# One 2 MB weight load requested as 32 partitions and 96 partitions

## The chip, the cores and the metric

The kernel runs on one core of a Trainium2 chip. The time is device microseconds of one execution, the median of several runs. The span in a profile is about 2 us shorter (77.6 us in a run of 79.66). In the profile's lines, PE is the matrix engine's matmuls and PEld its weight loads, DVE, ACT and POOL are the vector, scalar and general engines, and SP issues most requests. A request is one DMA instruction. A bulk request gives 16 completion increments in these traces, read here as one from each DMA engine whose share has landed.

## The reference, cut to what matters

```python
xn = layernorm(x)                                   # one token, D = 512
q  = xn @ wq                                        # wq: 512 x 4096, 4 MB
# 32 query heads, 8 key/value heads, the last W = 4096 positions of a cache of 65536
o  = softmax(q k^T / sqrt(128)) v
out = x + o @ wo + xn + sigmoid(xn . w_r) * ((silu(xn @ w_gate) * (xn @ w_up)) @ w_down)
```

One token meets 30.7 MB of weights and cache rows. Each is read once, so there is little arithmetic per byte.

## The kernel before

`wq` lies as [128 partitions, 4 rows, 4096]. Its first half is 16 KB per partition. The request for it, and the one for `x`, are moved by hand to the start of the program, ahead of the barrier that all engines pass ("the head barrier"). They reach SP and ACT as their first instructions.

```python
    KH = KT // 2                                              # 2
    wq_v = A_wq.rearrange("(p kt) n -> p kt n", kt=KT)
    ...
            for i in [i for i, o in enumerate(blk.instructions) if o.name in ahead][::-1]:
                ins = blk.instructions.pop(i)
                at = next(k for k, o in enumerate(head) if o.engine == ins.engine and isinstance(o, mybir.InstDrain))
                head.insert(at, ins)
    ...
    t_wq = [early(nc.sync, "wq0", wq_sb[:, 0:KH, :], wq_v[:, 0:KH, :])]       # ahead of the barrier
    t_x = early(nc.scalar, "x", xrow[:], A_x.rearrange("a b d -> (a b) d"))
    ...
    t_wq.append(dma(sy, "wq1", wq_sb[:, KH:, :], wq_v[:, KH:, :]))            # behind it
    t_k = sum([pair("k", k_sb, A_k_cache, a, b) for a, b in steps([0, 1, 2, 4, 6, 8])], [])
    ...
    for kh in range(2):
        PE.need(t_wq[kh], t_ps0)                              # the projection waits for its half of wq
    ...
    # then v, w_gate, w_up, wo, w_down, all from SP, long ahead of their use
```

## Time and profile before

| | |
|---|---|
| time, median of 3 | 79.57 us (79.53 to 79.73) |
| span in the profile | 77.6 us |
| moved from HBM | 30.67 MB, 395 GB/s over the span |
| first packet of wq | 1.04 us |
| last completion increment of w_down | 75.61 us |

The first thing to look at is the page's row of GB/s in 40 slices of 1.94 us, here of the kernel before:

```profile
GB/s 136 405 406 422 414 422 427 422 469 414 439 456 439 405 422 414 439 439 431 405 410 422 481 414 422 413 449 399 451 406 451 413 422 414 481 361 413 355 29 1
```

The row is flat from its second entry to the last three. This kernel ends when its bytes have passed: 30.67 MB at some 425 GB/s are 72 of its 77.6 us. For the experiments below, the same in three stretches of the kernel before (length, busy time and number of instructions of PE, PEld, DVE, ACT and POOL, PE's granted clock, DMA share, GB/s):

```profile
2.00:7.00 5.00, 0.26 (x4) 0.21 (x4) 2.76 (x6) 2.72 (x5) 2.89 (x5) 1.00 0.99 420
7.00:11.00 4.00, 2.80 (x20) 1.01 (x20) 2.81 (x14) 0.20 (x1) 0.00 (x0) 1.00 0.99 426
11.00:16.00 5.00, 3.56 (x26) 1.07 (x24) 0.60 (x5) 1.17 (x2) 0.00 (x0) 1.00 0.99 418
```

The first stretch is wq's first half, the second its second half, the third the first cache rows. All three move 418 to 426 GB/s with the DMA share at 0.99.

### The profile page before, as it was taken

To read this page: it belongs to the slowest core of one execution; us is meant where nothing else is said; L and a number is where in the kernel's file an instruction comes from. 1 tells how busy PE (TensorE), PEld (TensorE's weight loads), DVE (VectorE), ACT (ScalarE), POOL (GpSimd) and SP (SyncE) were. 2 spreads that over 40 slices of the span, in tenths; PEclk is the share of its full clock that TensorE was granted. 3 is DMA by queue.
4 is the path that set the end of the run, shared out by engine and by line. 5 is a ranking of instruction groups with operands and counts; after the bars stand their busy time and mean duration, and the time that the engine had idled before them with its cause. 6 is when DMAs were issued, how large, how long until landed. Compare 5 with 4: busy or idle time off the path is not lost.

```text
span 77.6 us, 1640 instructions
## 1 busy us (share of the span) xinstructions
PE 58.4 (75%) x642; PEld 30.6 (39%) x642; DVE 44.2 (57%) x96; ACT 30.4 (39%) x41; POOL 10.0 (13%) x22
## 2 busy tenths in 40 slices
PE   0010797759997997997996796677887889898891
PEld 0010401346785575765864234222222344243240
DVE  2763910177656956868883652989879545600302
ACT  2760101404397698599568016143333322000001
POOL 3950000001020210201205900000000000000000
PEclk9999999999999999999999999999999999999999
DMA  6999999999999999999999999999999999989900
GB/s 136 405 406 422 414 422 427 422 469 414 439 456 439 405 422 414 439 439 431 405 410 422 481 414 422 413 449 399 451 406 451 413 422 414 481 361 413 355 29 1
DMA packets 2745, 30.72 MB, mean 396 GB/s; under 512 B 307, under 2 KB 438, under 8 KB 822
## 3 DMA queue, kind: packets, MB, share of 16 engines
q1 hardware_dynamic: 2738, 30.67, 94.0%
q8 instruction: 2, 0.03, 0.2%
q14 instruction: 1, 0.01, 0.0%
q10 hardware_dynamic: 4, 0.00, 0.0%
HBM read 30.67 MB, written 0.00 MB: 395 GB/s over the span
## 4 chain that ended last, share of the span: by engine, by line
DMA 64%; PE 20%; ACT 6%; DVE 4%; issue 2%; SPq 1%
DMA k_sb<-in_B_w_down_dram 50%; DMA wq_sb<-in_A_wq_dram 14%; PE ps L367 10%; ACT kT L342 6%; PE ps L541 3%; PE ps L376 3%; PE ps L295 2%; DVE kin L334 2%; PE ps L307 1%; SPq L199 1%; DVE kT L339 1%; DVE qpad L312 1%; DVE kT L568 1%; SPq L84 0%; SPq L101 0%
## 5 line engine op out<-in xcount | busy, mean ns | idle before, releaser
L342 ACT COPY kT<-ps 128x1024 bf16<-128x1024 bf16 x19 | 18.6, 1016 | 9.5 <-PE ps L367 9.4
L367 PE MATMUL ps<-perm_bf,kin 128*128 128x128 bf16 x256 | 18.7, 231 | 1.5 <-DVE kin L334 1.0
L367 PEld LDWEIGHTS ps<-perm_bf,kin 128*128 128x128 bf16 x256 | 15.8, 104 | 5.9 <-issue 4.7
L334 DVE COPY kin<-k_sb 128x2048 bf16<-128x2048 bf16 x16 | 10.9, 687 | 2.6 <-PE ps L367 2.6
L339 DVE COPY kT<-ps 128x1024 bf16<-128x1024 bf16 x13 | 9.0, 692 | 4.4 <-PE ps L367 3.8
L462 ACT CAST pvS<-ps 128x512 bf16<-128x512 f32 x8 | 4.7, 586 | 10.0 <-PE ps L468 10.0
L376 PE MATMUL ps<-kT,qAB 128*32 128x512 bf16 x68 | 7.1, 407 | 1.9 <-ACT kT L342 1.9
L191 PE MATMUL ps<-zmov,zst 128*128 128x512 bf16 x32 | 7.9, 381 | 0.0
L327 POOL COPY qAB<-qpad 128x64 bf16<-128x64 bf16 x8 | 3.6, 445 | 32.6 <-PE ps L376 32.6
L442 DVE COPY vin<-v_sb 128x2048 bf16<-128x2048 bf16 x8 | 5.5, 685 | 1.1 <-PE ps L477 0.9
L448 DVE COPY vin<-v_sb 128x2048 bf16<-128x2048 bf16 x8 | 5.5, 683 | 0.0
L477 PE MATMUL ps<-vin,pTcur 128*32 128x512 bf16 x32 | 3.2, 386 | 2.6 <-ACT pvS L462 2.2
L569 ACT CAST kT<-ps 1x256 bf16<-1x256 f32 x1 | 0.4, 362 | 11.4 <-PE ps L541 11.4
L489 PE MATMUL ps<-zmov,zst 128*128 128x512 bf16 x16 | 4.7, 376 | 0.0
L295 PE MATMUL ps<-wq_sb,xnT 128*1 128x512 bf16 x32 | 3.8, 620 | 0.6 <-DMA wq_sb<-in_A_wq_dram 0.6
L191 PEld LDWEIGHTS ps<-zmov,zst 128*128 128x128 bf16 x32 | 2.7, 97 | 3.7 <-issue 1.3
L251 PE MATMUL ps<-ident_bf,xn_row 1*128 1x1 bf16 x4 | 0.3, 166 | 5.2 <-DVE xn_row L246 5.2
L312 DVE COPY qpad<-ps 128x16 bf16<-128x16 bf16 x4 | 0.5, 170 | 5.4 <-PE ps L307 5.4
L555 DVE TENSOR_TENSOR kT<-ps,kT 128x512 f32<-128x512 f32 x1 | 0.7, 692 | 5.0 <-PE ps L536 5.0
L376 PEld LDWEIGHTS ps<-kT,qAB 128*32 128x32 bf16 x68 | 1.9, 93 | 4.1 <-issue 1.8
L477 PEld LDWEIGHTS ps<-vin,pTcur 128*32 128x32 bf16 x32 | 1.1, 93 | 6.0 <-DVE vin L442 5.5
L483 PE MATMUL ps<-vin,pTcur 128*32 128x512 bf16 x32 | 3.2, 387 | 0.3 <-DVE vin L448 0.2
(96 smaller groups left out, 54.7 us busy)
## 6 DMA issues: line engine op xcount, KB each, us to landing
v_sb<-in_A_v_cache_dram SPq DMA_DIRECT2D x4, 2048.0 KB, 38.2
k_sb<-in_A_k_cache_dram SPq DMA_DIRECT2D x3, 2048.0 KB, 23.3
wq_sb<-in_A_wq_dram SPq DMA_DIRECT2D x2, 2048.0 KB, 9.1
k_sb<-in_A_wo_dram SPq DMA_DIRECT2D x2, 2048.0 KB, 34.7
k_sb<-in_A_k_cache_dram SPq DMA_DIRECT2D x2, 1024.0 KB, 13.9
wq_sb<-in_B_w_gate_dram SPq DMA_DIRECT2D x1, 1792.0 KB, 43.0
wq_sb<-in_B_w_up_dram SPq DMA_DIRECT2D x1, 1792.0 KB, 46.9
k_sb<-in_B_w_down_dram SPq DMA_DIRECT2D x1, 896.0 KB, 38.7
```

Source lines behind the costliest of these rows:

```text
L191: te.matmul(ps[:, 7, :], lhsT=zst[:], rhs=zmov[:], start=True, stop=True)
L295: ins = te.matmul(ps[32 * c:32 * c + 1, hf, :], lhsT=xnT[:, kt:kt + 1], rhs=wq_sb[:, kt, (4 * hf + c) * 512:(4 * hf + c + 1) * 512], start ...
L334: ve.tensor_copy(out=kin[:, 2 * h:2 * h + 2, :], in_=k_sb[:, g, 2 * h:2 * h + 2, :]).then_inc(s_c[h], 1)
L339: ve.tensor_copy(out=kT[:, b, :], in_=tp[:, b, :]).then_inc(s_ev[b], 1)
L342: ac.copy(out=kT[:, b, :], in_=tp[:, b, :]).then_inc(s_ev[b], 1)
L367: ins = te.transpose(tp[:, b, k * P:(k + 1) * P], kin[:, b, k * P:(k + 1) * P], perm_bf[:])
L376: ins = te.matmul(sc[32 * cq:32 * cq + 32, e, :], lhsT=qAB[:, e, :], rhs=kT[:, b, :].rearrange("d (k h q) -> d h k q", h=2, q=PH)[:, e], s ...
L442: ve.tensor_copy(out=vin[:, 0].rearrange("p (q k) d -> p q (k d)", q=4), in_=v_in[:, :, 0:4 * DH]).then_inc(s_va, 1)
L448: ve.tensor_copy(out=vin[:, 1].rearrange("p (q k) d -> p q (k d)", q=4), in_=v_in[:, :, 4 * DH:]).then_inc(s_vb, 1)
L462: ac.copy(out=pvS[:].rearrange("p t d -> p (t d)"), in_=pv_ps).then_inc(s_pvs, 1)
L477: ins = te.matmul(pv_ps[32 * tl:32 * tl + 32, :], lhsT=pTcur[:, tl].rearrange("p q e r -> p (q e r)"), rhs=vin[:, 0].rearrange("p (q t) d ...
L489: te.matmul(ps[:, 7, :], lhsT=zst[:], rhs=zmov[:], start=True, stop=True)
```

## The change

The intent is a smaller first request, so that its first packets start earlier, with the rest requested right behind it. The bytes and their places stay the same.

```diff
-                at = next(k for k, o in enumerate(head) if o.engine == ins.engine and isinstance(o, mybir.InstDrain))
+                at = next(k for k, o in enumerate(head) if o.engine == ins.engine and (isinstance(o, mybir.InstDrain) or o.name in ahead))
@@
-    t_wq = [early(nc.sync, "wq0", wq_sb[:, 0:KH, :], wq_v[:, 0:KH, :])]
+    t_wq0 = [early(nc.sync, f"wq0{a}", wq_sb[a:b, 0:KH, :], wq_v[a:b, 0:KH, :]) for a, b in ((0, 32), (32, P))]
@@
-    t_wq.append(dma(sy, "wq1", wq_sb[:, KH:, :], wq_v[:, KH:, :]))
+    t_wq = [t_wq0, [dma(sy, "wq1", wq_sb[:, KH:, :], wq_v[:, KH:, :])]]
@@
-        PE.need(t_wq[kh], t_ps0)
+        PE.need(*t_wq[kh], t_ps0)
```

The first line of the diff keeps the two requests in order. SP has one request more, and PE one wait more, since its projection now needs two semaphores. On the other engines the program is the same, instruction by instruction.

## The prediction

The sum came to between -0.5 and about +1.9 us. Two of its terms are 1.2 us for the first piece and up to another 1.2 us for the second, for slower packets to fewer partitions; +1.9 is both of them less 0.5. They were an assumption that no trace showed: every bulk request in the trace of the kernel before covers all 128 partitions. Rival (c) is this loss. The last sentence of Step 4 holds in that trace: the engine that was 1.44 us behind at 33.26 us was 1.42 us behind at 75.61, and the kernel ended by it.

> **What bounds the kernel now.** I read the page's busy tenths first, then the chain of waits, then the timeline of the first two and the last four microseconds, and last the stretches of DMA traffic between them.
>
> ```profile
> span 77.6 us, 1640 instructions
> ...
> PE 58.4 (75%) x642; PEld 30.6 (39%) x642; DVE 44.2 (57%) x96; ACT 30.4 (39%) x41; POOL 10.0 (13%) x22
> ...
> DMA  6999999999999999999999999999999999989900
> ...
> HBM read 30.67 MB, written 0.00 MB: 395 GB/s over the span
> ...
> DMA 64%; PE 20%; ACT 6%; DVE 4%; issue 2%; SPq 1%
> ```
>
> No compute engine is busy over 75%, while the 16 DMA engines are full from the first slice to slice 36. The chain that ended last consists 64% of two waits for transfers, wq at the start and w_down at the end. Its middle (the transposes) only decides when SP may request wo and w_down, at 33.9 us; w_gate and w_up were still landing then (57.1 and 61.4 us by their completion increments), so the queue never ran dry and that middle does not set the time. The stretches say it in numbers:
>
> ```profile
> 0.00:1.00 1.00, 0.00 (x0) 0.00 (x0) 0.00 (x0) 0.00 (x0) 0.20 (x4) 1.00 0.00 0
> 1.00:2.00 1.00, 0.00 (x0) 0.00 (x0) 0.47 (x3) 0.55 (x1) 0.52 (x3) 1.00 1.18 263
> 2.00:3.00 1.00, 0.00 (x0) 0.00 (x0) 1.00 (x2) 0.94 (x2) 1.00 (x4) 1.00 0.81 344
> 3.00:7.00 4.00, 0.26 (x4) 0.21 (x4) 1.76 (x5) 1.78 (x3) 1.89 (x3) 1.00 1.03 439
> 7.00:30.00 23.00, 18.88 (x202) 11.50 (x202) 13.30 (x34) 10.30 (x13) 1.77 (x4) 1.00 1.01 430
> 30.00:70.00 40.00, 33.82 (x383) 16.84 (x384) 26.57 (x53) 16.51 (x23) 4.65 (x7) 1.00 1.00 425
> ```
>
> The last column is GB/s. From 3 us to 70 us it is flat at 425 to 439. What an earlier start can win lies in the first three rows: nothing in the first microsecond, 263 in the second, 344 in the third. In the records of single packets a 16,384-byte packet takes 0.611 us in the steady part, and an engine carries 30.67 MB / 16 = 1.92 MB = 117 such packets, or 71.5 us. The first packets of the 16 engines start at 1.04 to 1.79 us and all end at 2.16 to 2.62, 0.69 to 1.52 us each. An engine that ran at 0.611 us from 1.04 us on would end its first packet at 1.65, so some 0.5 to 1.0 us per engine is spent on the ramp, and 1.04 us before it on the request.
>
> ```profile
> 0.00 0.41 SPq L105 DMA_DIRECT2D wq_sb<-in_A_wq_dram  x1
> 0.12 0.50 ACTq L105 DMA_DIRECT2D xrow<-in_A_x_dram  x1
> ...
> 1.27 0.33 SPq L199 DMA_DIRECT2D wq_sb<-in_A_wq_dram  x1
> ...
> 75.33 0.09 PEld L541 LDWEIGHTS ps<-k_sb,hTr 128*1 128x1 bf16 x4 [0.31 <-DMA k_sb<-in_B_w_down_dram]
> 75.65 0.08 PEld L541 LDWEIGHTS ps<-k_sb,hTr 128*1 128x1 bf16 x2 [0.23 <-DMA k_sb<-in_B_w_down_dram]
> 75.97 0.36 ACT L569 CAST kT<-ps 1x256 bf16<-1x256 f32 x1 [11.42 <-PE ps L541]
> 75.97 0.41 DVE L568 CAST kT<-ps 1x256 bf16<-1x256 f32 x1 [2.96 <-PE ps L541]
> 76.41 0.32 SPq L199 DMA_DIRECT2D out_dram<-kT  x1
> ```
>
> At the end the last w_down piece releases two weight loads at 75.65, then matmul, copy and store take the rest, 1.95 us, whatever came before. Which DMA engine is last matters. A transfer gives 16 completion increments. Those of the last piece come at 73.82 to 74.19 us for fourteen of them, at 75.13 for one and at 75.61 for one. The last engine falls behind in the seventh transfer: 15 increments by 31.82 us, the last at 33.26. An instruction-fetch packet of 16,384 bytes ran from 30.63 for 1.06 us, so I take it that one data engine also fetches instructions and loses 1.44 us to it. The kernel ends by that one engine. Each other engine has about 1.4 us of slack (0.5 us for the second late one).
>
> [...] the trace has 0.63 us from the end of the first request to the first packet, and 0.42 us for the one-row output store (request ends 76.74, packet at 77.16). [...]
>
> **The change part by part.** Removed: one request of 128 rows of 16,384 bytes. Added: requests of 32 and 96 such rows, in that order, both ahead of the barrier. Bytes are the same.
>
> Step 1, SP's issue time. Requests cost 0.41 and 0.33 us for 128 rows, 0.32 for one row, so the cost is per request. SP is then free at about 0.41 + 0.35 = 0.76 us, its drain takes 0.12, and it reaches the barrier near 0.9. In before the last to arrive was ACT, its drain ended at 0.80. So the barrier opens about 0.1 us later and everything behind it starts 0.1 us later. That costs nothing: the second half of wq is requested at some 1.4 us, and the engines have wq0 until 6.5 to 6.9; the compute start has slack, since its second projection waits for wq1 until 12.13 (idle 0.62 us on PE, 1.5 us on the weight loads).
>
> Step 2, an earlier first packet. If the descriptors of 128 rows are what spreads the starts over 1.04 to 1.79 us, a quarter of them takes about 0.19 us. A bound on the front: the one-row store took 0.75 us from request to packet, against 1.04, so at best 0.29 us there. The first packets would start at 0.8 to 1.0 and end at 1.7 to 2.1. Gain: 0.3 to 0.6 us.
>
> Step 3, no hole between the pieces. Two packets last 1.2 us from there, to 2.3 or later; the second piece, requested at 0.41, should have packets ready at 0.41 + 1.04 = 1.45 to 2.2. Just enough. Later boundaries between transfers cost nothing visible: the fifth transfer's increments are 4.89 us after the fourth's, eight packets of 0.611.
>
> [...] An engine that loses time never gets it back; what counts is the engine that ends last.
>
> Step 5, PE waits on two semaphores rather than one: one instruction at 8.7 us, where both had long landed (7.25). Nothing.
>
> Sum: between -0.5 us (steps 1 and 2 alone) and about +1.9 (all of step 4 less 0.5). If the lost time falls on engines with 1.4 us of slack, even the worst case shows as about +0.7 (1.2 lost by all less 0.5).
>
> **The rivals.** (a) Earlier start, passed through to the end: -0.3 to -0.6 us, 79.0 to 79.3. For it: a saturated queue with no idle slice. Against: early first packets took longest (1.04 + 1.14, but 1.79 + 0.69, end within 0.3 us of each other), as if something common held them. (b) That common thing, a slow ramp of reads or a fixed request latency, stays: 0 to -0.2 us, 79.4 to 79.6. For it: requests cost the same for 1 and 128 rows, and x, one row, had its packet only at 1.38. (c) [...] +0.7 to +1.9, 80.3 to 81.5. [...] against: only 0.5 MB is concerned, and the slack of most engines hides part. (d) Step 3 fails and the 96-row request comes late: a hole of 0.1 to 0.5 us, which eats the gain: 79.5 to 79.8.
>
> **Range and chances.** I give (a) 0.3, (b) and (d) together 0.35, (c) 0.35. Weighted: 0.3 x 79.15 + 0.35 x 79.55 + 0.35 x 80.7 = 79.8; the likelier values are below the mean, so I say 79.7, with 79.0 to 81.0. Two per cent is 1.59 us. Faster by that is more than the whole ramp: 0.01. Slower by that needs nearly all of (c) on the late engine: 0.08. Within: 0.91.
>
> **What would show it right or wrong.** Step 1: SP's third request near 1.4 us. Step 2: the first packets before 1.0 us, their ends before 2.1. Step 3: no packets missing between the second and third of an engine. Step 4: packets of the first piece at 1.2 us rather than 0.61 in the steady part, and wq0's last increment after 7.25 us. The end: last increment of w_down 75.61 plus the shift of the late engine, with 1.95 us behind it as before. The prediction is wrong if the late engine's instruction fetch moves or shrinks, up to 1.4 us not counted above, or if the queue starves in the middle.

## The result, and the profile after

The changed kernel takes 83.58 us (83.48 to 83.72, 5 runs) against 79.57 us (79.40 to 79.73, 5 runs) before: ratio 1.050, 95% interval 1.048 to 1.052. A ratio here is the mean time of one kernel's runs over that of the other's runs of the same rounds, so it is not quite the ratio of the medians. Executions over 1.5% slower than the fastest of the same kernel are left out of the means. The kernel is 5% slower, and 83.58 lies far outside the range of 79.0 to 81.0.

The page's row of GB/s of the changed kernel, in 40 slices of 2.04 us:

```profile
GB/s 129 257 241 241 201 345 409 413 422 430 470 417 409 458 418 409 458 418 409 458 397 409 466 401 418 466 388 446 436 414 416 469 401 418 466 374 404 392 58 1
```

Entries two to five are 201 to 257, where before they were 405 to 422. From the seventh on, the rows are alike. The dent is right at the start, and it is as long as wq's first half. The three stretches again, now of the changed kernel:

```profile
2.00:7.00 5.00, 0.26 (x4) 0.21 (x4) 2.89 (x6) 2.94 (x5) 3.25 (x6) 1.00 1.08 252
7.00:11.00 4.00, 0.02 (x1) 0.03 (x1) 1.04 (x5) 0.20 (x1) 0.00 (x0) 1.00 0.89 209
11.00:16.00 5.00, 3.40 (x20) 1.02 (x20) 1.76 (x10) 0.00 (x0) 0.00 (x0) 1.00 0.97 413
```

The DMA share stays near 1 while the rate is 252 and 209. So the engines are not waiting for requests: packets are open and pass slowly. The records of single packets show how slowly. In order of their starts, packets 33 to 128 of wq's first half (each of the 16 engines carries eight, so these are mostly its third to eighth) take 1.13 us on average, against 0.618 us before. Summed over an engine's packets: the first is no longer than before (1.14 us against 1.18), the second takes 1.10 against 0.61, the third to eighth lose 0.51 each, and the ninth, already of the second half, takes 1.03 against 0.61. That is 3.9 us, and the span grew by 4.0 (77.6 to 81.6).

The requests and the end, from the timeline of the changed kernel (start, duration, engine, line, operation):

```profile
0.00 0.85 SPq L105 DMA_DIRECT2D wq_sb<-in_A_wq_dram  x2
...
1.48 0.35 SPq L199 DMA_DIRECT2D wq_sb<-in_A_wq_dram  x1
...
79.70 0.08 PEld L541 LDWEIGHTS ps<-k_sb,hTr 128*1 128x1 bf16 x2 [0.23 <-DMA k_sb<-in_B_w_down_dram]
...
80.46 0.31 SPq L199 DMA_DIRECT2D out_dram<-kT  x1
```

The last w_down piece releases its weight loads at 79.70, 4.05 us later than before, and the rest of the kernel follows it at the same distance. All 16 engines are late: the last piece's first fourteen increments come at 78.01 to 78.47 us (before: 73.82 to 74.19), the last at 79.66 (75.61). The early start did not appear. The first packets start at 1.02 to 1.93 us and end at 2.20 to 2.75. Before, they started at 1.04 to 1.79 and ended at 2.16 to 2.62.

### The profile page after: what moved, and what is told of

Same layout as the page of the kernel before. It is cut to its first block, busy times and chain, and to the rows that moved or that the text cites. A ratio compares the mean times of both kernels' runs of the same rounds, so it can differ in the third digit from the quotient of the medians.

```text
span 81.6 us, 1642 instructions
## 1 busy us (share of the span) xinstructions
PE 59.2 (73%) x642; PEld 31.3 (38%) x642; DVE 44.1 (54%) x96; ACT 30.6 (37%) x41; POOL 10.2 (12%) x22
## 4 chain that ended last, share of the span: by engine, by line
DMA 65%; PE 23%; ACT 4%; DVE 3%; issue 1%; SPq 1%
DMA k_sb<-in_B_w_down_dram 47%; DMA wq_sb<-in_A_wq_dram 18%; PE ps L367 12%; ACT kT L342 4%; PE ps L376 4%; PE ps L541 3%; PE ps L295 2%; DVE kin L334 1%; PE ps L307 1%; SPq L199 1%; DVE kT L339 1%; DVE qpad L312 1%; DVE kT L568 1%; SPq L84 0%; SPq L101 0%
## 5 line engine op out<-in xcount | busy, mean ns | idle before, releaser
L367 PE MATMUL ps<-perm_bf,kin 128*128 128x128 bf16 x256 | 19.4, 237 | 1.4 <-DVE kin L334 0.9
L367 PEld LDWEIGHTS ps<-perm_bf,kin 128*128 128x128 bf16 x256 | 16.5, 106 | 6.0 <-issue 4.8
L266 PE MATMUL ps<-sml,ones_f 1*128 1x1 f32 x2 | 0.6, 359 | 5.4 <-DVE sml L264 5.4
L301 ACT CAST q<-ps 128x512 bf16<-128x512 f32 x2 | 1.2, 585 | 7.0 <-PE ps L295 7.0
```

Source lines behind the costliest of these rows:

```text
L367: ins = te.transpose(tp[:, b, k * P:(k + 1) * P], kin[:, b, k * P:(k + 1) * P], perm_bf[:])
```

## The experiments

The theory after this reading is that it is the write side: a request that covers few partitions has packets of about twice the time (1.13 us against 0.618). How that would come about no run shows; the words of the expectations that say it are cut from them, and what follows such a cut is what this theory expects. The rivals:

- the second request or the later barrier,
- the cold start of the core,
- the side that reads HBM,
- the number of rows as such.

Each edit is against the changed kernel. The runs of the kernel before that go with them had medians of 79.59 to 79.69 us (79.30 to 80.45).

**Two requests, both over all partitions.** The same proportion, 0.5 MB and 1.5 MB, cut along the row:

```diff
-    t_wq0 = [early(..., wq_sb[a:b, 0:KH, :], wq_v[a:b, 0:KH, :]) for a, b in ((0, 32), (32, P))]
+    t_wq0 = [early(..., wq_f[:, a:b], wq_s[:, a:b]) for a, b in ((0, 2048), (2048, 8192))]   # 2-D views of the same half
```

> Two requests ahead of the barrier in the same proportion, 0.5 MB and 1.5 MB, but both over all 128 partitions (4 KB and 12 KB of each row). [...] the slow start is gone, 79.6 us, within 0.3 of before. Rival, the second request ahead of the barrier or the later barrier costs it: as slow as the changed kernel, about 83.6 us.

Measured: 79.47 us (79.44 to 79.52), ratio 0.996 (0.989 to 1.003), correct. The first two stretches of this kernel:

```profile
2.00:7.00 5.00, 0.26 (x4) 0.21 (x4) 2.91 (x6) 2.95 (x5) 3.27 (x6) 1.00 1.05 436
7.00:11.00 4.00, 2.59 (x19) 1.00 (x20) 2.80 (x14) 0.20 (x1) 0.00 (x0) 1.00 1.04 446
```

The dent is gone. SP issues its third request at 1.50 us, as late as in the changed kernel (1.48). So neither the second request nor the later barrier costs anything. What is left is how the pieces are cut: which partitions they cover, or which rows they read.

**The second half of wq cut by partitions instead.** The first half is one request again. The other is behind the barrier, in a running stream:

```diff
-    ... for a, b in ((0, 32), (32, P))]                        # first half
+    ... for a, b in ((0, P),)]
-    t_wq = [t_wq0, [dma(sy, "wq1", wq_sb[:, KH:, :], wq_v[:, KH:, :])]]
+    t_wq = [t_wq0, [dma(sy, f"wq1{a}", wq_sb[a:b, KH:, :], wq_v[a:b, KH:, :]) for a, b in ((0, 32), (32, P))]]
```

> wq's first half in one request as before, its second half (behind the barrier, in the running stream) as 32 and 96 partitions. [...] the same 4 MB... of it the 2 MB of this half run at half rate, +4 us, 83.6 us, and 16 KB packets of some 1.1 us while it runs. Rival, a cold start or the barrier: 79.6 us, packets of 0.61 us.

Measured: 84.01 us (83.98 to 84.27), ratio 1.054 (1.046 to 1.062). The three stretches of this kernel:

```profile
2.00:7.00 5.00, 0.26 (x4) 0.21 (x4) 2.76 (x6) 2.71 (x5) 2.89 (x5) 1.00 1.03 420
7.00:11.00 4.00, 2.37 (x19) 0.93 (x20) 2.80 (x14) 0.20 (x1) 0.00 (x0) 1.00 1.02 229
11.00:16.00 5.00, 0.99 (x6) 0.08 (x2) 0.00 (x0) 0.00 (x0) 0.00 (x0) 1.00 0.96 215
```

The first stretch is at 420 again, and the dent has moved with the cut to 7 us and later, at 229 and 215. Packets of the cut half take 1.12 us on average. A cold start or the place ahead of the barrier cannot explain this. The span grew by 4.5 us. Those eight packets of each engine lost 4.05 us in sum, and the first packets of the cache rows right behind them (8 KB) lost 0.4.

**The same partitions, other source rows.** The two requests read rows of the key cache, 36 KB apart, in place of rows of wq, 32 KB apart.

```diff
+    src_v = A_k_cache[0, 0, 0:144 * P, :].rearrange("(r t) d -> r (t d)", t=144)[:, 0:8192].rearrange("r (a b) -> r a b", a=KH)
-    ... wq_v[a:b, 0:KH, :]
+    ... src_v[a:b]
```

> Wrong result on purpose: the two requests write the same 32 and 96 partitions but read rows of another tensor 36 KB apart. [...] still 83.6 us, first 128 packets at 1.1 us. Rival, the read side (which rows of wq the 16 engines read together): back to about 79.6 us.

Measured: 83.70 us (83.54 to 83.86), ratio 1.049 (1.041 to 1.057); packets 33 to 128 take 1.13 us on average, as in the changed kernel. (The comparison with the reference passed all the same. Presumably the query hardly moves the output within the tolerance. So it says nothing about the values of wq, here or in any other run.) Its first two stretches:

```profile
2.00:7.00 5.00, 0.26 (x4) 0.21 (x4) 2.98 (x6) 2.93 (x5) 3.11 (x6) 1.00 1.11 259
7.00:11.00 4.00, 0.00 (x0) 0.00 (x0) 0.21 (x1) 0.00 (x0) 0.00 (x0) 1.00 0.87 205
```

**The same source rows, all partitions.** The mirror image: four requests of 32 source rows of wq each, every row dealt as four pieces of 4 KB over four partitions.

```diff
+    t_wq0 = [early(..., wq_f[:, 2048 * s:2048 * (s + 1)],
+                   wq_s[32 * s:32 * (s + 1), :].rearrange("r (c n) -> r c n", c=4)) for s in range(4)]
```

> Wrong result on purpose: 32 source rows at a time, the same read pattern as the first request, but each row is dealt as four 4 KB pieces over 4 partitions, so that each of four requests writes all 128. [...] full rate, 79.6 us, up to 0.5 more for four requests ahead of the barrier. Rival, the read side or few source rows: 83.6 us or more.

Measured: 80.59 us (80.31 to 80.61; one run of 81.72 was slow), ratio 1.008 (0.998 to 1.018). Packets of 4 KB take 0.159 us, which for 16 KB is 0.64. So the packets run at full rate, and the read side is cleared from this side too. The time is 0.5 us above what I expected. The four requests cost SP 0.6 us each, the first packet starts at 1.42 us, the requests land 1.25 to 1.45 us apart where full rate gives 1.2, and one engine falls 1.0 us behind in the third request. Why that engine does so stays open; the trace has no instruction fetch at that time.

**64 and 64 partitions.**

```diff
-    ... for a, b in ((0, 32), (32, P))]
+    ... for a, b in ((0, 64), (64, P))]
```

> Partitions 0 to 63 and 64 to 127 in two requests. [...] half rate all through, 83.6 us. Rival, only the odd sizes 32 and 96 are slow (two and six rows per engine): 79.6 us.

Measured: 84.79 us (84.69 to 84.84), ratio 1.062 (1.055 to 1.069): slow as expected, and 1.2 us beyond. Packets 33 to 128 take 1.25 us on average, and the first nine packets of an engine lost 4.7 us in sum. The first packet starts 0.33 us later, as the requests took SP 0.58 us each. Together that is 5.0 us; the span grew by 5.3, and the rest I did not trace.

**32, 64 and 32 partitions.** The run that separates "which partitions" from "how many". The middle request has 64 rows like those above, but it lies across the middle, on partitions 32 to 95:

```diff
-    ... for a, b in ((0, 32), (32, P))]
+    ... for a, b in ((0, 32), (32, 96), (96, P))]
```

The expectation gives two outcomes of the theory, in this order: the first if each engine writes four neighbouring rows of the middle request, the second if rows are dealt out 32 at a time. No trace records which.

> Partitions 0 to 31, 32 to 95, 96 to 127 in three requests. [...] the middle one [...] runs at 0.61 us per packet; the outer ones at 1.1; loss half of the change's, about 81.6 us. [...] the middle one is slow too, 83.6 us. Rival, any request of under 128 rows is slow: 83.6 us as well.

Measured: 82.30 us (82.18 to 82.45), ratio 1.032 (1.025 to 1.039). The stretches of this kernel while each of the three requests runs, and after them:

```profile
1.50:4.00 2.50, 0.00 (x0) 0.00 (x0) 1.42 (x4) 1.48 (x2) 1.47 (x5) 1.00 1.10 269
4.50:6.50 2.00, 0.26 (x4) 0.21 (x4) 1.24 (x2) 1.77 (x3) 1.45 (x2) 1.00 1.01 418
7.00:9.00 2.00, 0.00 (x0) 0.00 (x0) 0.00 (x0) 0.00 (x0) 0.00 (x0) 1.00 1.00 230
10.00:13.00 3.00, 2.34 (x19) 0.90 (x20) 2.31 (x14) 0.20 (x1) 0.00 (x0) 1.00 1.03 437
```

The middle request runs at 418 GB/s, the outer ones at 269 and 230. Partitions 0 to 63 and 64 to 127 are slow, while 32 to 95, equally many rows in requests of the same size, run at full rate. The number of rows is cleared. The first of the three expectations held in kind; the time was 0.7 us above the 81.6 named.

**Eight engines for the 32 partitions.** With its source written as 8 groups of 4 rows and a gap between them, the first request gets 8 completion increments from data, so 8 engines carry it.

```diff
+    src8 = wq_v[:, 0:KH, :].rearrange("(a b) kt n -> a b (kt n)", a=8)[:, 0:4, :]
-    ... wq_sb[0:32, 0:KH, :], wq_v[0:32, 0:KH, :]
+    ... bass.AP(wq_sb, 0, [[KT * NQ, 32], [1, KH * NQ]]), src8
```

> Wrong result on purpose: the 32-partition request has its source written as 8 groups of 4 rows with a gap, so that only 8 engines carry it, four rows each. [...] its packets take 0.61 us in place of 1.1, and the request lasts as long as with 16 engines (2.5 us). Rival, every row of a short request is slow by itself: packets of 1.1 us, the request lasts 5 us. The time as a whole should be 83 to 85 us, as eight engines carry two packets more.

Measured: 84.43 us (84.02 to 84.82), ratio 1.059 (1.051 to 1.067), inside the 83 to 85 expected. Strung to engines by their ends and starts, the second to fourth packets of the eight engines take 0.61 to 0.83 us, median 0.62, where 16 engines on these 32 partitions took 1.1 each. The request spans from 1.61 us to its last increment at 5.55 us. That is longer than the 2.5 expected: its start was spread, and the other eight engines were already writing the second request. No run separates the two. The packets decide: a row of a short request is not slow by itself, and it is slow when 16 engines share these partitions. The stretches with eight engines on each request, and with all 16 on the second:

```profile
2.60:4.60 2.00, 0.00 (x0) 0.00 (x0) 1.60 (x4) 1.47 (x4) 2.00 (x5) 1.00 1.05 385
5.00:11.00 6.00, 0.36 (x5) 0.30 (x5) 1.99 (x8) 1.13 (x3) 0.58 (x2) 1.00 1.03 224
```

So the two requests ran side by side at 385 GB/s, and the 96-partition request became slow, at 224, when all 16 engines were on it. What the run does not show is how they share them. By an estimate from the packet times, eight engines at 0.62 us a packet bring 211 GB/s into partitions 0 to 31, and 16 at 1.13 bring 232, so a limit of about that size on these partitions as a whole would fit.

**Four requests of 32 partitions.** Why were all six packets of the 96-partition request slow (1.13 us), when its rows lie on both sides of partition 64, as do those of 32 to 95, which ran at 418 GB/s?

```diff
-    ... for a, b in ((0, 32), (32, P))]
+    ... for a, b in ((0, 32), (32, 64), (64, 96), (96, P))]
```

> Four requests of 32 partitions each. In the changed kernel all six packets of the 96-partition request took 1.13 us, as if its rows were dealt out 32 at a time, two neighbours per engine. If so, three requests of 32 in its place are the same thing: eight packets of 1.1 us on every engine, wq0 last landed within 0.5 us of the changed kernel's 11.76 us, 83.6 to 84.2 us. If the 96 rows were slow for another reason (six in a block per engine, an odd size), the requests of 32 differ from it by over 1 us.

Measured: 84.44 us (84.16 to 84.53), ratio 1.059 (1.054 to 1.065). The first half of wq has landed at 12.23 us against 11.76, but packets 33 to 128 take 1.25 us on average against 1.13, and the time is above the range that I named. So 96 partitions in one request behave nearly, not exactly, like three times 32. Which engine writes which row is not recorded, and the run with eight engines speaks against the dealing expected here. Dealt 32 at a time in order, the second request's first rows would lie in partitions 32 to 63, on the same side as the first request's 0 to 31. All of 0 to 63 took 16 KB packets of about 1.25 us from 16 engines in the run of 64 and 64, some 210 GB/s, yet there the two requests moved 385 together. So why the whole 96-partition request is slow stays open.

**Does a column cut win anything?** The first experiment again with more rounds, and with a first piece of half the size:

> The column split again, to see whether its 0.1 us earlier last landing holds: 79.4 to 79.6 us, 0.1 to 0.3% under before; the interval will probably include equality.

> A first request of half the size, 2 KB of each row. If a smaller first piece over all partitions helps the ramp: 79.4 us or less. If the first packet's start at 1.0 us is a fixed latency: 79.4 to 79.6 us, the same.

Measured: 79.40 us (79.34 to 79.66), ratio 0.998 (0.994 to 1.002), and 79.57 us (79.35 to 79.78), ratio 0.999 (0.994 to 1.003). The first packets start at 1.02 us in both. The column cut costs nothing and wins nothing that these runs can tell from zero; no version here beats the kernel before.

## Why the prediction was wrong

- **What bounds the kernel** was right. A loss of 4.0 us in the first 11 us of the DMA stream reached the end in full, although PE, DVE and ACT idled more and the middle chain ran 4.3 to 4.6 us later. The 1.95 us behind the last w_down piece stayed.
- **Step 1, the issue time**, was right in kind. SP's third request came 0.21 us later and not 0.1, since the second request cost 0.41 us where 0.35 was assumed, and 0.04 us lay between the two. The column cut, with the same delay, showed that this is free.
- **Step 2, an earlier first packet**, was wrong. A gain of 0.3 to 0.6 us was assumed if the descriptors of 128 rows spread the starts. With 32 rows the first packet came at 1.02 us and the spread was no smaller. That is rival (b): the first packet did not come earlier for fewer rows. (It can come later: at 1.36 us for requests of 64 rows, each of which took SP 0.58 us.)
- **Step 3** was right: there is no hole between the pieces. In the changed kernel each engine's third packet starts at most 0.003 us after its second has ended.
- **Step 4, slower packets to fewer partitions**, is the step that failed, and it failed by size. Its first term was right: the 32-partition request landed at 4.83 us, where the same 0.5 MB over all partitions (the first column cut) landed at 3.41, so it lost 1.4 us where 1.2 was named. Its second term gave the 96-partition request up to another 1.2 us, from a count over all its rows that was an assumption. The runs showed all six packets slow on every engine, 6 x (1.13 - 0.62) = 3.1 us. The landings say the same: 11.76 - 4.83 = 6.9 us for the 96-partition request, against 7.12 - 3.41 = 3.7 for the column cut's 1.5 MB. That count does not describe this; what does stays open, as said above.
- **The slack** was the second part of that error. The argument that lost time might fall on engines with 1.4 us to spare needed an uneven loss. All sixteen lost four microseconds: the increments of the last piece came 4.05 to 4.28 us later.
- **The chances** followed from these. Rival (c) got 0.35 and a worst case of +1.9, with "only 0.5 MB is concerned" against it. It concerned 2 MB. (The working also has a slip: the middle of (c), 80.3 to 81.5, is 80.9 and not 80.7, which makes the weighted mean 79.9.) With the second term at 3.1 us, the same working would have given 1.2 + 3.1 - 0 = +4.3 us.

## What to carry to other kernels

Cut a transfer along the row and keep all 128 partitions in each piece: such a cut was free here (79.40 to 79.57 us against 79.59 to 79.69), while a cut by partitions put a full DMA stream at about half its rate for as long as the pieces ran (252 and 209 GB/s against 420 and 426), with one exception, the piece over partitions 32 to 95 (418 GB/s). When judging where a transfer lands, do not trust a count over the whole transfer: partitions 32 to 127 lie on both sides of 64, and in the changed kernel their request was slow from its first packet to its last (1.13 us each). A DMA share near 1 does not mean full rate (1.08 at 252 GB/s); read the GB/s beside it, or the duration of a packet.
